# LayerNorm's reciprocal deviation on GpSimd, and more of the normalising on ScalarE

## The chip, the cores and the metric

The kernel runs on one core of one Trainium2 chip. The metric is the device time of one launch in microseconds, the median of several runs; the profile is of one further execution, and its span is a little shorter than the time. A core has five engines with instruction queues of their own: TensorE (PE: matmuls and weight loads), VectorE (DVE), ScalarE (ACT), GpSimd (POOL) and SyncE (SP, which here only issues DMAs). They meet through semaphores.

## The reference

The input x has 2048 tokens of 576 values. A LayerNorm (epsilon 1e-5) feeds a linear attention block with 32 heads of 18 channels; a gated feed-forward block of width 4608 works on the same normalised tokens, as the last lines say:

```
x = A_x
xn = _layernorm(x, axis=-1)
return x + _A_ref(xn, A_wqkv, A_wo) + _B_ref(xn, B_w_gate, B_w_up, B_w_down)
```

Attention computes q, k, v from xn, phi(t) = where(t > 0, t + 1, exp(t)) + 1e-6 for q and k, a 18x18 sum of phi(k) times v per head, the sum z of phi(k), and the quotient of the two products with phi(q), times wo. The change concerns only how (x - mean) / sqrt(var + eps) is made.

## The kernel before

The tokens lie as 16 tiles of 128. The work has three stages. The first, up to about 58 us of the profile, takes each tile through the LayerNorm, transposes it, multiplies it with the key and query weights, forms phi and adds the tile to a product G of xn and phi(k). A short second stage, up to 66.7 us, finishes the sums and the masked attention matrices. The third, to the end, is the feed-forward block with the attention output folded into its last product; it takes up the rest of the span and isn't touched.

The path of tile n in the first stage, by the names in the code:

- stats and aggr (L211, L214, VectorE): two halves of mean and variance, then joined into mv.
- rstd (`ln_rstd`, L216 to L219, ScalarE): 1/sqrt(var + eps) as exp(-0.5 ln(var + eps)), two activations on one value per partition.
- norm: on VectorE (`ln_norm`, L231) as (x - mean) * rstd; or on ScalarE (`ln_norm_act`, L226) as x * rstd + nbias, for which GpSimd first makes nbias = -mean * rstd (`ln_bias`, L221). Odd tiles from 3 on take ScalarE, the others VectorE.
- the transpose: tiles 0 and 1 go over PE (`transposes`, L244) in two parts, blocks 0 to 2 and blocks 3 and 4 of the 128 columns, each part with its own norm and its own copy back (`tp_copy`, L249, line L251). The later tiles take a DMA transpose issued by SP (`dma_transposes`, L253).
- mm, exp, phi (L262, L269, L274): per tile two halves of the key product and two of the query product, each five matmuls of 288 columns, an exponential on ScalarE and a combination on VectorE. A tile's product reuses the bank of the tile before, so it waits for that phi.
- z (`z_add`, GpSimd, L197) sums phi(k), and G (L293, PE) accumulates.

The order of the instructions on each engine is not written out by hand. Each of these is a step with an engine, a planned duration, a rank, and the steps that it follows; `in_order` (L482) plays the steps through with the planned durations and, among what could begin within 0.05 us, picks the lowest rank on that engine. So a planned duration or another engine moves instructions of other tiles as well. On the chip the queues then run strictly in that order, with the real durations.

Ahead of the steps, the loads are issued: tile 0 and 1 of x, the key weights (`load_w(1)`), two more tiles, the query weights (`load_w(0)`), four more tiles. PE runs 38 small products on an identity (`spin`) while it waits. GpSimd fills constants: padding of xn, ones in the bias rows, and the masks of the second stage (`bmask` L179 to L187, a part of `g_sb` L189, `ones` L192).

Of the kernel before, what the change touches and what calls it, by code (L numbers as in the profile page):

```python
# [8 lines left out]
ACT = mybir.ActivationFunctionType  # L9
ALU = mybir.AluOpType  # L10
BF16 = mybir.dt.bfloat16
F32 = mybir.dt.float32
# [3 lines left out]
P = 128  # L16
HP = 64
S = 2048
D = 576
H = 32  # L20
DH = 18
F = 4608
NS = S // P
# [5 lines left out]
KT = 5  # L29
# [4 lines left out]
EPS_LN = 1e-5  # L34
# [23 lines left out]
def kernel(  # L58
# [11 lines left out]
    nc = tc.nc  # L70
# [8 lines left out]
    const = ctx.enter_context(tc.tile_pool(name="const", bufs=1))  # L79
# [10 lines left out]
    x_sb = persist.tile([P, NS, D], BF16, name="x_sb")  # L90
# [28 lines left out]

    ident = const.tile([P, P], BF16, name="ident")  # L120
    make_identity(nc, ident[:])
    eps_ln = const.tile([P, 1], F32, name="eps_ln")
    nc.vector.memset(eps_ln[:], EPS_LN)
    eps_att = const.tile([P, 1], F32, name="eps_att")
    nc.vector.memset(eps_att[:], EPS_ATT)
    neg1 = const.tile([P, 1], F32, name="neg1")
    nc.vector.memset(neg1[:], -1.0)

    def spin(count):

        for _ in range(count):
            nc.tensor.matmul(ps_all[:, 7, 0:P], lhsT=ident[:], rhs=ident[:], start=True, stop=True)
# [19 lines left out]
    def load_gu(i, part):  # L152
# [17 lines left out]
    xn = apool.tile([P, NS, XW], BF16, name="xn")  # L170
# [4 lines left out]
    nc.gpsimd.memset(pk[:, :, D + 1:D + 2], 1.0)  # L175

    bmask = const.tile([P, CR], F32, name="bmask")
    bm3 = bmask[:].rearrange("p (h e) -> p h e", e=DH)
    nc.gpsimd.memset(bmask[:], 1.0)  # L179
    nc.gpsimd.affine_select(  # L180
        out=bm3, in_=bm3, compare_op=ALU.is_ge, fill=0.0,
        base=0, pattern=[[-DH, 7], [0, DH]], channel_multiplier=1,
    )
    nc.gpsimd.affine_select(
        out=bm3, in_=bm3, compare_op=ALU.is_ge, fill=0.0,
        base=DH - 1, pattern=[[DH, 7], [0, DH]], channel_multiplier=-1,
    )  # L187
    g_sb = apool.tile([P, KT, D], BF16, name="g_sb")
    nc.gpsimd.memset(g_sb[:, 4, :], 0.0)  # L189

    ones = const.tile([P, P], BF16, name="ones")
    nc.gpsimd.memset(ones[:], 1.0)  # L192
    z_sum = apool.tile([P, D], F32, name="z_sum")
    z_bf = apool.tile([P, D], BF16, name="z_bf")

# [6 lines left out]
    mv = persist.tile([P, NS, nc.vector.BN_AGGR_DIM], F32, name="mv")  # L202
    rstd = persist.tile([P, NS], F32, name="rstd")
    nbias = persist.tile([P, NS], F32, name="nbias")
# [3 lines left out]
    def ln_half(n, h):  # L208
        if h == 0:
            ln_raw[n] = asmall.tile([P, 2, nc.vector.BN_STATS_DIM], F32, name="stats")  # L210
        nc.vector.bn_stats(out=ln_raw[n][:, h, :], in_=x_sb[:, n, h * HALF:(h + 1) * HALF])  # L211

    def ln_aggr(n):
        nc.vector.bn_aggr(out=mv[:, n, :], in_=ln_raw[n][:])  # L214

    def ln_rstd(n):  # L216
        r = rstd[:, n:n + 1]
        nc.scalar.activation(out=r, in_=mv[:, n, 1:2], func=ACT.Ln, bias=eps_ln[:], scale=1.0)
        nc.scalar.activation(out=r, in_=r, func=ACT.Exp, scale=-0.5)  # L219

    def ln_bias(n):  # L221
        nc.gpsimd.tensor_scalar(
            out=nbias[:, n:n + 1], in0=mv[:, n, 0:1], scalar1=rstd[:, n:n + 1], scalar2=-1.0, op0=ALU.mult, op1=ALU.mult,
        )

    def ln_norm_act(n):  # L226
        nc.scalar.activation(
            out=xn[:, n, 0:D], in_=x_sb[:, n, :], func=ACT.Identity, bias=nbias[:, n:n + 1], scale=rstd[:, n:n + 1],
        )

    def ln_norm(n, c0=0, c1=D):  # L231
        nc.vector.tensor_scalar(
            out=xn[:, n, c0:c1], in0=x_sb[:, n, c0:c1], scalar1=mv[:, n, 0:1], scalar2=rstd[:, n:n + 1],
            op0=ALU.subtract, op1=ALU.mult,
        )
# [8 lines left out]
    def transposes(n, k0=0, k1=KT, b=None):  # L244
        b = TP_BANK[n] if b is None else b
        for kt in range(k0, k1):
            nc.tensor.transpose(tp_bank(b)[:, kt, :], xn[:, n, kt * P:(kt + 1) * P], ident[:])

    def tp_copy(n, k0=0, k1=KT, b=None, copy=acopy):  # L249
        b = TP_BANK[n] if b is None else b  # L250
        copy(out=xnT[:, k0:k1, n * P:(n + 1) * P], in_=tp_bank(b)[:, k0:k1, :])  # L251

    def dma_transposes(n):  # L253
        nc.sync.dma_start_transpose(xnT[:, :, n * P:(n + 1) * P], xn[:, n, 0:640])
# [4 lines left out]
    def kq_mm(n, which, hf):  # L259
        c = which * D + hf * HALF  # L260
        for kt in range(KT):
            nc.tensor.matmul(  # L262
                ps_all[:, KQ_BANK[which] + hf, :HALF], lhsT=xnT[:, kt, n * P:(n + 1) * P],
                rhs=wqkv_sb[:, kt, c:c + HALF], start=(kt == 0), stop=(kt == KT - 1),
            )

    def kq_exp(n, which, hf):
        e = e_tiles[n, which, hf] = awork.tile([P, HALF], F32, name="phi_e", tag="phi_e", bufs=8)
        nc.scalar.activation(  # L269
            out=e[:], in_=ps_all[:, KQ_BANK[which] + hf, :HALF], func=ACT.Exp, bias=neg1[:], scale=1.0,  # L270
        )
# [159 lines left out]
    def step(name, *args, **kw):  # L431
        steps[name] = _Step(*args, **kw)

    X_AT = [3.65, 4.20, 6.40, 6.40] + [9.50] * 4
    W_AT = {1: 5.50, 0: 7.60}

# [2 lines left out]
    for n in range(NS):  # L439
        lead = {0: -9.0, 1: 0.5, 2: -0.5, 3: -0.5}.get(n, 0.0)  # L440
        after_x = [("x", n // 2 * 2)] if n >= 8 else []
        x_at = X_AT[n] if n < 8 else 0.0
        for h in range(2):
            step(("stats", n, h), "DVE", 0.41, n - 2.2 + lead, after_x, lambda n=n, h=h: ln_half(n, h), ready=x_at)
        step(("aggr", n), "DVE", 0.21, n - 2.1 + lead, [("stats", n, 0), ("stats", n, 1)], lambda n=n: ln_aggr(n))
        step(("rstd", n), "ACT", 0.49, n - 2.1 + lead, [("aggr", n)], lambda n=n: ln_rstd(n))
        if n < TD:
            for i, (k0, k1, eng) in enumerate([(0, 3, "ACT"), (3, KT, "ACT" if n else "DVE")]):
                b = TP_BANK[n] - i
                step(("norm", n, i), "DVE", 0.25, n - 2.1 + lead, [("rstd", n)],  # L450
                     lambda n=n, k0=k0, k1=k1: ln_norm(n, k0 * P, min(k1 * P, D)))
                step(("tp", n, i), "PE", 0.20, n - 1.5 + lead, [("norm", n, i)],
                     lambda n=n, k0=k0, k1=k1, b=b: transposes(n, k0, k1, b))
                step(("xnT", n, i), eng, 0.30 if i else 0.48, n - 0.88 + lead, [("tp", n, i)],
                     lambda n=n, k0=k0, k1=k1, b=b, eng=eng: tp_copy(n, k0, k1, b, acopy if eng == "ACT" else vcopy))
            ready = [("xnT", n, 0), ("xnT", n, 1)]
        else:
            if n % 2:
                step(("bias", n), "POOL", 0.15, n - 2.1, [("rstd", n)], lambda n=n: ln_bias(n))
                step(("norm", n), "ACT", 0.65, n - 2.1, [("bias", n)], lambda n=n: ln_norm_act(n))  # L460
            else:
                step(("norm", n), "DVE", 0.43, n - 2.1, [("rstd", n)], lambda n=n: ln_norm(n))
            step(("xnT", n), "SP", 2.10, n - 1.9, [("norm", n)], lambda n=n: dma_transposes(n), tail=1.7)
            ready = [("xnT", n)]
        for which, rank in ((1, n), (0, n + 0.6)):
            for h in range(2):
                r = rank + h / 100
                free = [("phi", n - 1, which, h)] if n else []
                step(("mm", n, which, h), "PE", 0.615, r, ready + free, lambda n=n, w=which, h=h: kq_mm(n, w, h),
                     ready=W_AT[which], tail=0.15)  # L470
                step(("exp", n, which, h), "ACT", 0.49, r + 0.10, [("mm", n, which, h)],
                     lambda n=n, w=which, h=h: kq_exp(n, w, h))
                step(("phi", n, which, h), "DVE", 0.44, r + 0.15, [("exp", n, which, h)],
                     lambda n=n, w=which, h=h: kq_phi(n, w, h))
        if n > 0:
            idle = [("norm", n + 4) if n % 2 == 0 else ("bias", n + 4)] if n + 4 < NS else []
            step(("z", n), "POOL", 1.40, n + 2.0, [("phi", m, 1, h) for m in (0, n) for h in range(2)] + idle,
                 lambda n=n: z_add(n))
        step(("G", n), "PE", 0.75, n + 1.15, [("phi", n, 1, 0), ("phi", n, 1, 1)], lambda n=n: g_accumulate(n, G_A))
    step(("spin",), "PE", 0.11, -1.0, [("tp", 0, 1)], lambda: spin(2))  # L480

    def in_order(steps):  # L482

# [262 lines left out]
```

## Time and profile before

The time is 512.57 us, the median of 3 runs (512.55 to 512.6); the profile's span is 510.9 us.

| engine | busy us | share of the span | instructions |
|---|---|---|---|
| PE matmul | 505.0 | 99% | 4487 |
| PE weight load | 305.4 | 60% | 4487 |
| VectorE | 211.2 | 41% | 447 |
| ScalarE | 136.8 | 27% | 267 |
| GpSimd | 24.7 | 5% | 38 |

The operations that the change touches, in the first stage:

| line, engine | operation | count | mean ns |
|---|---|---|---|
| L218 ACT | Ln, 128x1 | 16 | 288 |
| L219 ACT | Exp, 128x1 | 16 | 203 |
| L222 POOL | nbias, 128x1 | 7 | 265 |
| L227 ACT | norm, 128x576 | 7 | 862 |
| L232 DVE | norm, 128x576 | 7 | 439 |
| L232 DVE | norm, 128x384 and 128x192 | 2 and 2 | 352 and 323 |
| L197 POOL | z sum, 128x576 | 13 | 1244 |

A matmul's reported length includes its way through the pipeline, so consecutive ones overlap; its cost to the next is the distance of their starts. The chain of work that ended last is followed back from the last instruction: at each step to what released it. What is busy beside that chain costs nothing. In a timeline line the first number is the start in us, the second the time that the group spans, and the bracket says how long the engine was idle before it and what ended that.

### The profile page before, as it was taken

The page shows a single profiled execution, that of the slowest core. Times are in us where ns is not written, and L with a number is a line of the kernel's source. Part 1 is how long each engine was busy: PE and PEld are TensorE (multiplying, and loading weights), DVE is VectorE, ACT ScalarE, POOL GpSimd, SP SyncE. Part 2 cuts the span into 40 slices and gives each one's busy share as a digit, 9 for nine tenths or more (in the row PEclk, how much of TensorE's full clock was granted, in tenths as well). Part 3 has the DMA queues.
Part 4 walks back from the last instruction along what each step waited for, and adds up shares of the span by engine and source line. Part 5 has one row for each costly group of instructions (what it writes and reads, how often), then busy time and mean ns, then how long its engine had stood idle before and what let it go on. Part 6 is the DMA issues. An engine that isn't in the chain of part 4 may idle for free.

```text
span 510.9 us, 10642 instructions
## 1 busy us (share of the span) xinstructions
PE 505.0 (99%) x4487; PEld 305.4 (60%) x4487; DVE 211.2 (41%) x447; ACT 136.8 (27%) x267; POOL 24.7 (5%) x38
## 2 busy tenths in 40 slices
PE   7999999999999999999999999999999999999997
PEld 6888854444587744444677644444777444445775
DVE  7887455555400045565200255555100356543100
ACT  5887533332310022332100023323000232232000
POOL 3344200000000000000000000000000000000000
PEclk9999999999999999999999999999999999999999
DMA  6643939999500067665300266567100565540000
GB/s 210 144 66 56 256 94 262 279 272 289 136 12 13 1 175 168 158 167 161 87 12 13 69 172 170 156 172 157 32 12 1 148 166 156 164 129 14 13 12 24
DMA packets 119002, 61.26 MB, mean 120 GB/s; under 512 B 25570, under 2 KB 118122, under 8 KB 118954
## 3 DMA queue, kind: packets, MB, share of 16 engines
q1 hardware_dynamic: 118810, 60.43, 45.3%
q8 instruction: 35, 0.57, 0.5%
q10 hardware_dynamic: 144, 0.15, 0.1%
q14 instruction: 13, 0.11, 0.1%
HBM read 52.86 MB, written 2.36 MB: 108 GB/s over the span
## 4 chain that ended last, share of the span: by engine, by line
PE 98%; DMA 1%; SPq 0%; DVE 0%; issue 0%
PE ps_all L324 55%; PE ps_all L668 28%; PE ps_all L262 7%; PE ps_all L293 3%; PE ps_all L673 3%; DMA wqkv_sb<-in_A_wqkv_dram 1%; PE ps_all L656 0%; PE ps_all L300 0%; PE ps_all L373 0%; PE ps_all L619 0%; SPq L93 0%; SPq L108 0%; DVE res L682 0%; SPq L107 0%; PE ps_all L361 0%
## 5 line engine op out<-in xcount | busy, mean ns | idle before, releaser
L324 PE MATMUL ps_all<-xnT,wg 64*128 64x512 bf16 x1152 | 271.9, 376 | 0.0
L324 PE MATMUL ps_all<-xnT,wu 64*128 64x512 bf16 x1152 | 271.5, 376 | 0.0
L608 ACT ACTIVATE gl<-ps_all 128x512 f32<-128x512 f32 x144 | 86.0, 597 | 311.1 <-PE ps_all L324 311.1
L609 DVE TENSOR_TENSOR hT<-ps_all,gl 128x512 bf16<-128x512 f32 x144 | 99.6, 691 | 131.2 <-ACT gl L608 130.7
L324 PEld LDWEIGHTS <-wu 64*128 64x128 bf16 x1152 | 108.3, 94 | 68.3
L324 PEld LDWEIGHTS <-wg 64*128 64x128 bf16 x1152 | 108.3, 94 | 67.7
L668 PE MATMUL ps_all<-wd_sb,hT 128*128 128x288 bf16 x1152 | 147.1, 286 | 0.0
L668 PEld LDWEIGHTS <-hT 128*128 128x128 bf16 x1152 | 112.3, 98 | 29.3 <-issue 1.2
L682 DVE TENSOR_TENSOR res<-ps_all,x_sb 128x288 bf16<-128x288 f32 x32 | 13.8, 455 | 146.4 <-PE ps_all L673 88.2
L324 PE MATMUL ps_all<-xnT,wr 64*128 64x512 bf16 x288 | 54.6, 376 | 0.0
L262 PE MATMUL ps_all<-wqkv_sb,xnT 128*128 128x288 bf16 x320 | 42.1, 286 | 0.5 <-ACT xnT L251 0.3
L262 PEld LDWEIGHTS <-xnT 128*128 128x128 bf16 x320 | 30.5, 98 | 7.9 <-ACT xnT L251 0.4
L269 ACT ACTIVATE phi_e<-ps_all,neg 128x288 f32<-128x288 f32 x64 | 30.9, 495 | 9.1 <-PE ps_all L262 6.3
L324 PEld LDWEIGHTS <-wr 64*128 64x128 bf16 x288 | 14.0, 94 | 16.8 <-issue 0.2
L673 PE MATMUL ps_all<-m_sb,pqT 128*128 128x288 bf16 x128 | 20.9, 286 | 0.0
L293 PE MATMUL ps_all<-hT,xn 128*128 128x288 bf16 (+4 forms) x144 | 18.8, 274 | 0.0
L274 DVE SCALAR_TENSOR_TENSOR pq<-phi_e,ps_all 128x288 bf16<-128x288 f32 x32 | 14.2, 449 | 7.7 <-ACT phi_e L269 7.4
L197 POOL TENSOR_TENSOR z_sum<-z_sum,hT 128x576 f32<-128x576 f32 x13 | 16.2, 1244 | 4.7 <-DVE hT L274 4.4
L293 PEld LDWEIGHTS <-xn 128*128 128x128 bf16 x144 | 14.0, 98 | 3.6 <-issue 0.2
L274 DVE SCALAR_TENSOR_TENSOR hT<-phi_e,ps_all 128x288 bf16<-128x288 f32 x32 | 14.1, 453 | 2.4 <-ACT phi_e L269 2.3
L673 PEld LDWEIGHTS <-pqT 128*128 128x128 bf16 x128 | 12.5, 98 | 3.2
L211 DVE BATCH_NORM_STATS2 stats<-x_sb 128x6 f32<-128x288 bf16 x32 | 13.6, 440 | 1.8 <-DMA x_sb<-in_A_x_dram 1.8
(62 smaller groups left out, 123.3 us busy)
## 6 DMA issues: line engine op xcount, KB each, us to landing
wg<-in_B_w_gate_dram SPq DMA_DIRECT2D x72, 256.0 KB, 2.9
wu<-in_B_w_up_dram SPq DMA_DIRECT2D x72, 256.0 KB, 3.5
wd_sb<-in_B_w_down_dram SPq DMA_DIRECT2D x12, 432.0 KB, 4.7
wr<-in_B_w_gate_dram SPq DMA_DIRECT2D x72, 32.0 KB, 2.8
wr<-in_B_w_up_dram SPq DMA_DIRECT2D x72, 32.0 KB, 3.0
out_dram<-res SPq DMA_DIRECT2D x15, 144.0 KB, 1.8
wqkv_sb<-in_A_wqkv_dram SPq DMA_DIRECT2D x3, 576.0 KB, 4.6
x_sb<-in_A_x_dram SPq DMA_DIRECT2D x5, 288.0 KB, 3.2
```

The lines of the kernel that those rows point to most:

```text
L197: nc.gpsimd.tensor_tensor(out=z_bf[:] if n == NS - 1 else z_sum[:], in0=pk[:, 0, 1:D + 1] if n == 1 else z_sum[:], in1=pk[:, n, 1:D + 1], ...
L211: nc.vector.bn_stats(out=ln_raw[n][:, h, :], in_=x_sb[:, n, h * HALF:(h + 1) * HALF])
L262: nc.tensor.matmul(ps_all[:, KQ_BANK[which] + hf, :HALF], lhsT=xnT[:, kt, n * P:(n + 1) * P], rhs=wqkv_sb[:, kt, c:c + HALF], start=(kt == ...
L269: nc.scalar.activation(out=e[:], in_=ps_all[:, KQ_BANK[which] + hf, :HALF], func=ACT.Exp, bias=neg1[:], scale=1.0,)
L274: nc.vector.scalar_tensor_tensor(out=(pq, pk)[which][:, n, which + hf * HALF:which + (hf + 1) * HALF], in0=e_tiles[n, which, hf][:], scala ...
L293: nc.tensor.matmul(ps_all[:, b, col:col + w], lhsT=xn[:, n, kt * P:(kt + 1) * P], rhs=pk[:, n, 1 + d0:1 + d0 + w], start=(n == 0 and col = ...
L324: return nc.tensor.matmul(self.outs[i], lhsT=self.lhs(i, rows, kt), rhs=self.rhs(i, rows, kt), start=start, stop=stop, skip_group_check=True,)
L608: nc.scalar.activation(out=gl[:], in_=ps_all[:, b[0], :], func=ACT.Gelu_apprx_tanh)
L609: nc.vector.tensor_tensor(out=hT[:, GUB * k + i, :], in0=ps_all[:, b[1], :], in1=gl[:], op=ALU.mult)
L668: nc.tensor.matmul(self.acc(hf), lhsT=hT[:, f, j * P:(j + 1) * P], rhs=wd_sb[:, f, HALVES[hf]], start=(f == 0 and not paired), stop=False, ...
L673: nc.tensor.matmul(self.acc(hf), lhsT=pqT[:, c, self.ts], rhs=m_sb[:, c, HALVES[hf]], start=False, stop=(paired and c == 3), skip_group_ch ...
L682: nc.vector.tensor_tensor(out=self.res[:, hs], in0=self.acc(hf), in1=x_sb[:, self.n, hs], op=ALU.add)
```

## The change

The reciprocal deviation is made by GpSimd: an addition of epsilon, and a power with the exponent -0.5 held in a column `mhalf`. ScalarE no longer has Ln and Exp to do. Which engine normalises a tile is now written out in `NORM` (D for VectorE, A for ScalarE): tile 1 goes to ScalarE in its two parts, and of the later tiles 3, 5, 6, 7, 9, 10, 12, 13 and 15. The masks and constants of the second stage become steps for GpSimd that follow the third tile's rstd. The planner gets new durations for these steps. The aim is to take small dependent work off ScalarE and VectorE, and to let the first tiles reach PE sooner.

In the order of the built program, PE has all five transposes of tile 1 ahead of the first query matmuls of tile 0; before, three stood ahead of them and two between their halves.

```diff
--- before.py
+++ after.py
@@ -119,10 +119,10 @@
 
     ident = const.tile([P, P], BF16, name="ident")
     make_identity(nc, ident[:])
-    eps_ln = const.tile([P, 1], F32, name="eps_ln")
-    nc.vector.memset(eps_ln[:], EPS_LN)
     eps_att = const.tile([P, 1], F32, name="eps_att")
     nc.vector.memset(eps_att[:], EPS_ATT)
+    mhalf = const.tile([P, 1], F32, name="mhalf")
+    nc.vector.memset(mhalf[:], -0.5)
     neg1 = const.tile([P, 1], F32, name="neg1")
     nc.vector.memset(neg1[:], -1.0)
 
@@ -175,21 +175,25 @@
     nc.gpsimd.memset(pk[:, :, D + 1:D + 2], 1.0)
 
     bmask = const.tile([P, CR], F32, name="bmask")
-    bm3 = bmask[:].rearrange("p (h e) -> p h e", e=DH)
-    nc.gpsimd.memset(bmask[:], 1.0)
-    nc.gpsimd.affine_select(
-        out=bm3, in_=bm3, compare_op=ALU.is_ge, fill=0.0,
-        base=0, pattern=[[-DH, 7], [0, DH]], channel_multiplier=1,
-    )
-    nc.gpsimd.affine_select(
-        out=bm3, in_=bm3, compare_op=ALU.is_ge, fill=0.0,
-        base=DH - 1, pattern=[[DH, 7], [0, DH]], channel_multiplier=-1,
-    )
     g_sb = apool.tile([P, KT, D], BF16, name="g_sb")
-    nc.gpsimd.memset(g_sb[:, 4, :], 0.0)
-
     ones = const.tile([P, P], BF16, name="ones")
-    nc.gpsimd.memset(ones[:], 1.0)
+
+    def make_bmask():
+        bm3 = bmask[:].rearrange("p (h e) -> p h e", e=DH)
+        nc.gpsimd.memset(bmask[:], 1.0)
+        nc.gpsimd.affine_select(
+            out=bm3, in_=bm3, compare_op=ALU.is_ge, fill=0.0,
+            base=0, pattern=[[-DH, 7], [0, DH]], channel_multiplier=1,
+        )
+        nc.gpsimd.affine_select(
+            out=bm3, in_=bm3, compare_op=ALU.is_ge, fill=0.0,
+            base=DH - 1, pattern=[[DH, 7], [0, DH]], channel_multiplier=-1,
+        )
+
+    def clear_g():
+        nc.gpsimd.memset(g_sb[:, 4, :], 0.0)
+        nc.gpsimd.memset(ones[:], 1.0)
+
     z_sum = apool.tile([P, D], F32, name="z_sum")
     z_bf = apool.tile([P, D], BF16, name="z_bf")
 
@@ -215,17 +219,17 @@
 
     def ln_rstd(n):
         r = rstd[:, n:n + 1]
-        nc.scalar.activation(out=r, in_=mv[:, n, 1:2], func=ACT.Ln, bias=eps_ln[:], scale=1.0)
-        nc.scalar.activation(out=r, in_=r, func=ACT.Exp, scale=-0.5)
+        nc.gpsimd.tensor_scalar_add(out=r, in0=mv[:, n, 1:2], scalar1=EPS_LN)
+        nc.gpsimd.tensor_tensor(out=r, in0=r, in1=mhalf[:], op=ALU.pow)
 
     def ln_bias(n):
         nc.gpsimd.tensor_scalar(
             out=nbias[:, n:n + 1], in0=mv[:, n, 0:1], scalar1=rstd[:, n:n + 1], scalar2=-1.0, op0=ALU.mult, op1=ALU.mult,
         )
 
-    def ln_norm_act(n):
+    def ln_norm_act(n, c0=0, c1=D):
         nc.scalar.activation(
-            out=xn[:, n, 0:D], in_=x_sb[:, n, :], func=ACT.Identity, bias=nbias[:, n:n + 1], scale=rstd[:, n:n + 1],
+            out=xn[:, n, c0:c1], in_=x_sb[:, n, c0:c1], func=ACT.Identity, bias=nbias[:, n:n + 1], scale=rstd[:, n:n + 1],
         )
 
     def ln_norm(n, c0=0, c1=D):
@@ -431,6 +435,9 @@
     def step(name, *args, **kw):
         steps[name] = _Step(*args, **kw)
 
+    NORM = "DADADAAADAADAADA"
+    COPY = ("DVE", "ACT")
+    POW = 0.55
     X_AT = [3.65, 4.20, 6.40, 6.40] + [9.50] * 4
     W_AT = {1: 5.50, 0: 7.60}
 
@@ -443,19 +450,25 @@
         for h in range(2):
             step(("stats", n, h), "DVE", 0.41, n - 2.2 + lead, after_x, lambda n=n, h=h: ln_half(n, h), ready=x_at)
         step(("aggr", n), "DVE", 0.21, n - 2.1 + lead, [("stats", n, 0), ("stats", n, 1)], lambda n=n: ln_aggr(n))
-        step(("rstd", n), "ACT", 0.49, n - 2.1 + lead, [("aggr", n)], lambda n=n: ln_rstd(n))
+        step(("rstd", n), "POOL", POW, n - 2.1 + lead, [("aggr", n)], lambda n=n: ln_rstd(n))
         if n < TD:
-            for i, (k0, k1, eng) in enumerate([(0, 3, "ACT"), (3, KT, "ACT" if n else "DVE")]):
+            for i, (k0, k1, eng) in enumerate([(0, 3, "ACT"), (3, KT, COPY[n])]):
                 b = TP_BANK[n] - i
-                step(("norm", n, i), "DVE", 0.25, n - 2.1 + lead, [("rstd", n)],
-                     lambda n=n, k0=k0, k1=k1: ln_norm(n, k0 * P, min(k1 * P, D)))
+                if NORM[n] == "A":
+                    if not i:
+                        step(("bias", n), "POOL", 0.15, n - 2.1 + lead, [("rstd", n)], lambda n=n: ln_bias(n))
+                    step(("norm", n, i), "ACT", (0.49, 0.36)[i], n - 2.1 + lead, [("bias", n)],
+                         lambda n=n, k0=k0, k1=k1: ln_norm_act(n, k0 * P, min(k1 * P, D)))
+                else:
+                    step(("norm", n, i), "DVE", (0.27, 0.20)[i], n - 2.1 + lead, [("rstd", n)],
+                         lambda n=n, k0=k0, k1=k1: ln_norm(n, k0 * P, min(k1 * P, D)))
                 step(("tp", n, i), "PE", 0.20, n - 1.5 + lead, [("norm", n, i)],
                      lambda n=n, k0=k0, k1=k1, b=b: transposes(n, k0, k1, b))
                 step(("xnT", n, i), eng, 0.30 if i else 0.48, n - 0.88 + lead, [("tp", n, i)],
                      lambda n=n, k0=k0, k1=k1, b=b, eng=eng: tp_copy(n, k0, k1, b, acopy if eng == "ACT" else vcopy))
             ready = [("xnT", n, 0), ("xnT", n, 1)]
         else:
-            if n % 2:
+            if NORM[n] == "A":
                 step(("bias", n), "POOL", 0.15, n - 2.1, [("rstd", n)], lambda n=n: ln_bias(n))
                 step(("norm", n), "ACT", 0.65, n - 2.1, [("bias", n)], lambda n=n: ln_norm_act(n))
             else:
@@ -473,11 +486,14 @@
                 step(("phi", n, which, h), "DVE", 0.44, r + 0.15, [("exp", n, which, h)],
                      lambda n=n, w=which, h=h: kq_phi(n, w, h))
         if n > 0:
-            idle = [("norm", n + 4) if n % 2 == 0 else ("bias", n + 4)] if n + 4 < NS else []
+            idle = [("norm" if NORM[n + 4] == "D" else "bias", n + 4)] if n + 4 < NS else []
             step(("z", n), "POOL", 1.40, n + 2.0, [("phi", m, 1, h) for m in (0, n) for h in range(2)] + idle,
                  lambda n=n: z_add(n))
         step(("G", n), "PE", 0.75, n + 1.15, [("phi", n, 1, 0), ("phi", n, 1, 1)], lambda n=n: g_accumulate(n, G_A))
     step(("spin",), "PE", 0.11, -1.0, [("tp", 0, 1)], lambda: spin(2))
+
+    step(("bmask",), "POOL", 0.95, 0.2, [("rstd", 2)], make_bmask)
+    step(("g",), "POOL", 0.75, 0.3, [("rstd", 2)], clear_g)
 
     def in_order(steps):
```

## The prediction

> **What bounds the kernel now.** I read the page's busy shares first, then the chain that ended last, then the stages by window, then the timeline of the first ten microseconds. TensorE (PE) is busy 99% of the span, and the chain that ended last is 98% PE, so anything on another engine counts only where it makes PE wait. The windows say where that is. Columns: the stretch in us, its length, then PE, weight loads, VectorE, ScalarE and GpSimd busy time with counts, clock, DMA share, GB/s.
>
> ```profile
> 5.10:6.74 1.64, 0.64 (x7) 0.40 (x8) 1.38 (x7) 0.76 (x4) 0.36 (x2) 1.00 1.05 372
> 6.74:8.55 1.81, 1.57 (x14) 1.14 (x15) 1.74 (x7) 1.29 (x6) 0.00 (x0) 1.00 1.09 367
> 9.43:20.00 10.57, 10.57 (x91) 8.55 (x90) 9.55 (x27) 9.28 (x25) 2.70 (x4) 1.00 0.48 106
> 20.00:30.00 10.00, 10.00 (x87) 8.12 (x85) 9.15 (x28) 8.01 (x21) 3.78 (x6) 1.00 0.64 125
> 40.00:50.00 10.00, 10.00 (x86) 8.10 (x85) 7.01 (x19) 8.29 (x20) 5.34 (x6) 1.00 0.31 51
> ```
>
> From 9.43 to the feed-forward part PE has no idle time at all, although VectorE and ScalarE are busy 70 to 95% there. Time can be won or lost ahead of 9.43, or by a new gap later. The chain in order of time (start, length, what) shows what releases PE:
>
> ```profile
> 2.95 5.56 DMA wqkv_sb<-in_A_wqkv_dram
> 8.50 0.04 issue
> 8.55 0.77 PE ps_all L262 x5
> 9.32 0.11 PE ps_all L247 x2
> 9.43 1.84 PE ps_all L262 x15
> ```
>
> The query weights land at 8.50; five query matmuls of tile 0 start at 8.55; then two transposes of tile 1 (0.11 us) stand in the chain; then all is matmul. Behind 8.55 PE's work is fixed, so the end is 8.55 plus that work. The timeline shows tile 0 and 1 on their way there:
>
> ```profile
> 4.58 0.21 DVE L214 BATCH_NORM_AGGREGATE mv<-stats 128x2 f32<-128x12 f32 x1
> 4.83 0.30 ACT L218 ACTIVATE rstd<-mv,eps_ln 128x1 f32<-128x1 f32 x1 [2.31 <-DVE mv L214]
> 5.16 0.20 ACT L219 ACTIVATE rstd<-rstd 128x1 f32<-128x1 f32 x1
> 5.39 0.62 DVE L232 TENSOR_SCALAR xn<-x_sb,mv,rstd 128x384 bf16<-128x384 bf16 x2
> 5.93 0.20 DVE L214 BATCH_NORM_AGGREGATE mv<-stats 128x2 f32<-128x12 f32 x1
> 6.74 1.40 PE L262 MATMUL ps_all<-wqkv_sb,xnT 128*128 128x288 bf16 x10 [0.28 <-ACT xnT L251]
> 7.57 0.56 DVE L232 TENSOR_SCALAR xn<-x_sb,mv,rstd 128x384 bf16<-128x384 bf16 x2
> 7.98 0.33 PE L247 MATMUL ps_all<-ident,xn 128*128 128x128 bf16 x3
> ```
>
> Tile 1 was aggregated at 6.13, but its norm started only at 7.57, behind tile 2's statistics on VectorE. Hence only three of its five transposes fit before 8.55.
>
> **What the Trainium skill says.** (1) "ScalarE: Activation LUTs", section "What ACT_TABLE_LOAD costs": an ACTIVATE with a pointer bias takes about 280 ns + 0.833 ns per element, another pointer operand adds 93, neighbours overlap by 93. For the norm with two pointers and 576 columns that is 853 ns; the trace has 862, so it agrees. (2) "GPSIMD Engine Reference", section 3.1: a two-input operation costs about 2.6 cycles per element, at 1.2 GHz. The z sum over 576 columns would be 1.25 us by that; the trace has 1.244. It states no price for a power. (3) "Perfetto Trace Analysis", section "GPSIMD Engine Instruction": reported GpSimd spans are unreliable, start-to-start is better. Here the bias reads 0.265 us, yet the z sum behind it starts 0.22 after it. (4) "SBUF — State Buffer", section "Who interferes with whom": a VectorE tensor_scalar in a 2-port mode and a GpSimd operation exclude each other. The trace fits: the norm of 128x576 takes mostly 0.43 us, and 0.57 beside a z sum.
>
> **The change, part by part.**
>
> *Removed:* 16 pairs Ln+Exp on ScalarE, start to end 0.53 us each (4.83 to 5.36), 8.5 us of ScalarE. Behind 9.43 this is worth nothing: PE has no gap there. *Moved:* norms of tiles 6, 10 and 12 from VectorE (0.43) to ScalarE (0.86, 0.77 start to start), also behind 9.43 and hidden by PE; ScalarE nets about -6 us. *The masks* (1.7 us on GpSimd, 3.75 to 5.46) go behind the third rstd. They are read only at the mask product and the z product, about 66 us; hidden by 50 us of PE work. They cost the fourth tile's rstd a wait, treated below.
>
> *rstd on GpSimd.* Two instructions with a semaphore wait between them. The trace has no power. Lower bound: two of the cheapest 128x1 operations (memset, 0.10) with the 0.07 hand-off seen in the bmask chain: 0.27. Nearest row: the bias, 0.265, for each: 0.265+0.065+0.265 = 0.60. Upper bound: the page's two-input price says nothing of a function evaluated in software; for a power of about 1 us I take 1.4. I call the pair r and take 0.60, since one column leaves little but the fixed cost.
>
> *Tile 0's chain:* aggregate ends 4.79, GpSimd starts 4.83 and ends 4.83+r; before it was 5.36. So tile 0 shifts by d = r-0.53, 0.07 with my value. Its key matmuls start at 6.74+d and finish ten issues of 0.123 us at 7.97+d.
>
> *Tile 1's chain* (now on ScalarE): aggregate 6.13+d; rstd ends 6.17+d+r; bias with its hand-offs 0.065+0.265, ScalarE starts 0.04 later, at 6.54+d+r. What is queued behind these norms on ScalarE: two exps of tile 0, then the copies of tile 1's transposes. Norm halves by the page's formula (an estimate): 384 columns 0.69, next start 0.60 later, 192 columns 0.53, so the end is 1.13 later: 7.67+d+r. PE sees it 0.07 later and issues the last two transposes in 0.11. All five transposes now stand ahead of the first query matmul, so that matmul starts at the later of 8.55 (the weights, whose load isn't changed) and 7.85+d+r = 7.32+2r. With r = 0.60 this is 8.52, just inside. The two transposes then lie in the wait for the weights, and 0.11 us leaves the chain. Up to r = 0.615 the gain is the full 0.11; each 0.1 more costs 0.2; it breaks even at 0.67.
>
> *Behind that:* tile 1's copies end near 9.9 and its key matmuls need them from 9.78 (first three blocks, ready near 9.5) and 10.15: no stall. Tile 2: norm on VectorE at about 8.5, ends 8.92, DMA transpose issued 9.0, landing 2.6 us later at 11.6; PE needs it at 11.75 (11.86 less 0.11). That is tight, as before (9.06+2.6 = 11.66 against 11.86). Tile 3: rstd waits for the masks until about 10.2; norm 11.2 to 12.07, landing 14.7, needed 14.95; before it landed near 14.94 against 15.06. Tile 5's norm moves from 17.79 to about 17.1. GpSimd per tile: 0.60 + about 0.33 + 1.24 = 2.2 us of the 3.2 us that PE spends on a tile, so it holds.
>
> *Sum:* -0.11 us; 512.57 - 0.11 = 512.46, called 512.5.
>
> **The rivals.**
> - *The power costs more* (r from 0.67 to 1.18): the loss is 2r-1.34, from 0 to 1.0 us; at r = 0.9 it is 512.57+0.46 = 513.0. For it: a function of two operands in software. Against it: one element per partition, the rest of such rows is 0.1 to 0.27 us.
> - *The power is slow* (r over 1.18), and slower than before by over 0.2%: at r = 1.4 the loss is 1.46, 514.0; with r near 2 GpSimd reaches the 3.2 us per tile and becomes the bound. For it: no row and no page prices the operation. Against: it needs a power above 0.85 us, three times the bias.
> - *A late tile:* tile 2 or 3 misses its slack of 0.15 to 0.25 and PE stalls once, 0.1 to 0.4 us; 512.7. For it: the thin slack, and masks beside VectorE's norm. Against: ScalarE and VectorE both have less to do.
> - *A real gain* over 0.2% (1.03 us) would need the query weights earlier; their issue at 2.95 and the DMA share near 1.0 ahead of 8.55 aren't touched. About 511.5.
>
> **How the numbers follow.** My case 55%, costlier power 25%, slow power 12%, late tile 6%, real gain 2%. The time is that of my case, 512.5. Low end 512.3: the full gain, with the 0.05 us between runs and a little between chips; high end 513.4: r up to 1.1, which holds most of the second case and the fourth. Over 0.2% faster 2%; slower 13% (slow power and the edge of the second case); within it 85%.
>
> **What would show it.** In the chain of the changed kernel: the query weights' DMA still the piece before the first query matmul at 8.55, no transposes behind it. In GpSimd's timeline: start of the add to the end of the power 0.60. In ScalarE's: two norm pieces of tile 1 near 7.2 to 8.35. PE idle from there to 67 us: none. If the piece before the query matmuls is a transpose waiting for ScalarE's norm, the power was dearer; if a gap stands near 11.8 or 15, a tile came late; if GpSimd is busy all through, it became the bound.

## The result and the profile after

The changed kernel takes 514.88 us (median of 4 runs, 514.36 to 515.72) against 512.56 on the same chip: 2.3 us more, ratio 1.0048 with a 95% interval of 1.003 to 1.0065. The forecast was 512.5 with a range of 512.3 to 513.4, so the result lies outside. Its four runs stand on two levels, 514.36 and 514.38, 515.38 and 515.72, where the kernel before had all four within 0.25. The profiled run is one of the upper level.

TensorE now has idle time ahead of the feed-forward part. The page's head, and the share of each engine in the chain that ended last (98% PE before):

```profile
span 513.7 us, 10671 instructions
PE 507.6 (99%) x4487; PEld 306.8 (60%) x4487; DVE 211.3 (41%) x443; ACT 133.2 (26%) x239; POOL 38.3 (7%) x73
PE 93%; DVE 3%; POOL 1%; issue 1%; DMA 1%; ACT 1%; ACTq 0%
```

The first feed-forward matmul starts at 69.35, before at 66.61. These 2.74 us are nearly the whole 2.8 by which the span grew (510.9 to 513.7). A ruler between the two ends is the start of each tile's G matmuls (a G block), whose distance was 3.20 us before, up to the fifteenth. Some of these lines, before and after; those between are left out:

```profile
11.11 0.91 PE L293 MATMUL ps_all<-hT,xn 128*128 128x288 bf16 x7
27.11 0.92 PE L293 MATMUL ps_all<-hT,xn 128*128 128x288 bf16 x7
39.92 0.92 PE L293 MATMUL ps_all<-hT,xn 128*128 128x288 bf16 x7
```

```profile
12.61 0.91 PE L297 MATMUL ps_all<-hT,xn 128*128 128x288 bf16 x7
28.62 0.92 PE L297 MATMUL ps_all<-hT,xn 128*128 128x288 bf16 x7
32.15 0.92 PE L297 MATMUL ps_all<-hT,xn 128*128 128x288 bf16 x7
35.35 0.92 PE L297 MATMUL ps_all<-hT,xn 128*128 128x288 bf16 x7
38.95 0.91 PE L297 MATMUL ps_all<-hT,xn 128*128 128x288 bf16 x7
42.66 0.92 PE L297 MATMUL ps_all<-hT,xn 128*128 128x288 bf16 x7
```

In the changed kernel the first starts at 12.61 instead of 11.11 (**1.50 lost in the front**), and three distances, 28.62 to 32.15, 35.35 to 38.95 and 38.95 to 42.66, are longer by 0.33, 0.40 and 0.51 (**1.24 lost later**).

The front, by the chain in order of time (start, length, what):

```profile
5.05 0.24 POOL rstd L222
5.29 0.07 issue
5.36 0.58 POOL rstd L223
5.94 0.03 issue
5.97 0.39 DVE xn L236
6.36 0.05 issue
6.40 0.52 PE ps_all L251 x3
6.94 0.49 ACT xnT L255
7.43 0.05 issue
7.48 2.57 PE ps_all L266 x10
10.04 0.28 PE ps_all L251 x5
10.32 2.45 PE ps_all L266 x20
```

The DMA of the query weights is no longer the piece ahead of the query matmuls. The chain now comes from tile 0's statistics through both GpSimd instructions. From the add's start at 5.05 to the power's end at 5.94 are **0.89 us, not 0.60**; the power alone is 0.57. And the ten key matmuls of tile 0 take 2.57 us where the same ten took 1.40 before. The timeline of the changed kernel shows two paces of one row:

```profile
1.41 4.23 PE L132 MATMUL ps_all<-ident 128*128 128x128 bf16 x38 [1.41 <-POOL ident masks.py:199]
6.40 0.71 PE L251 MATMUL ps_all<-ident,xn 128*128 128x128 bf16 x5 [0.76 <-DVE xn L236]
7.48 2.57 PE L266 MATMUL ps_all<-wqkv_sb,xnT 128*128 128x288 bf16 x10
10.16 2.12 PE L266 MATMUL ps_all<-wqkv_sb,xnT 128*128 128x288 bf16 x16
```

At 7.48 one key matmul comes every 0.24 us, at 10.16 one every 0.12. Nothing waits in between: the array runs at half pace until about 10. The granted clock that the page prints is full all through.

The later loss, by the waits of ScalarE from 12 to 50 us (in total, times, longest). The kernel before had none for nbias:

```profile
ACT xn L231 <- POOL nbias L226: 5.2, 8, 1.2
ACT phi_e L273 <- PE ps_all L266: 2.5, 4, 1.2
```

One stall followed back, by the timeline of all engines:

```profile
28.16 0.21 DVE L218 BATCH_NORM_AGGREGATE mv<-stats 128x2 f32<-128x12 f32 x1
28.46 0.22 POOL L222 TENSOR_SCALAR rstd<-mv 128x1 f32<-128x1 f32 x1 [1.23 <-DVE mv L218]
28.77 0.57 POOL L223 TENSOR_TENSOR rstd<-rstd,mhalf 128x1 f32<-128x1 f32 x1
29.44 0.27 POOL L226 TENSOR_SCALAR nbias<-mv,rstd 128x1 f32<-128x1 f32 x1
29.74 0.87 ACT L231 ACTIVATE xn<-x_sb,nbias,rstd 128x576 bf16<-128x576 bf16 x1 [1.03 <-POOL nbias L226]
30.51 1.26 ACT L273 ACTIVATE phi_e<-ps_all,neg 128x288 f32<-128x288 f32 x3
31.03 0.46 DVE L278 SCALAR_TENSOR_TENSOR hT<-phi_e,ps_all 128x288 bf16<-128x288 f32 x1 [0.64 <-ACT phi_e L273]
31.54 0.77 PE L266 MATMUL ps_all<-wqkv_sb,xnT 128*128 128x288 bf16 x5 [0.17 <-DVE hT L278]
```

ScalarE's norm stands in its queue, 1.03 us idle, for a bias that GpSimd could not make sooner: from the aggregate's end at 28.37 to the bias's end at 29.71 are 1.34 us, where the order was written for 0.55 + 0.15 = 0.70. Behind the norm stand exponentials that don't depend on it. They come late, VectorE's phi products with them, then PE. GpSimd is idle 1.23 us ahead of this, so it isn't overloaded; each tile's chain through it is too long for the order. The aggregate at 28.16 is late itself, and GpSimd's z sums have a part in that: the tile before was aggregated at 24.54, but its add stood behind a z sum until 25.18, and its norm on VectorE, at 26.33, took 1.06 us beside the next z sum, ahead of the statistics that the aggregate needs.

So the theory had three parts: (a) the length of the power in front; (b) a low TensorE clock in some of the runs, because PE is idle too long between the spin and tile 0's transposes; (c) an order planned for a shorter power. The experiments take them one at a time. Times are medians with the range of the runs, ratios are to the kernel before (512.6 to 512.7) on the same chip.

### The profile page after: what moved, and what is told of

Same layout as the page of the kernel before. It is cut to its first block, busy times and chain, and to the rows that moved or that the text cites. A ratio compares the mean times of both kernels' runs of the same rounds, so it can differ in the third digit from the quotient of the medians.

```text
span 513.7 us, 10671 instructions
## 1 busy us (share of the span) xinstructions
PE 507.6 (99%) x4487; PEld 306.8 (60%) x4487; DVE 211.3 (41%) x443; ACT 133.2 (26%) x239; POOL 38.3 (7%) x73
## 4 chain that ended last, share of the span: by engine, by line
PE 93%; DVE 3%; POOL 1%; issue 1%; DMA 1%; ACT 1%; ACTq 0%
PE ps_all L328 54%; PE ps_all L684 28%; PE ps_all L266 4%; PE ps_all L689 3%; PE ps_all L297 2%; DVE pq L278 1%; DVE stats L215 1%; DVE hT L278 1%; DMA x_sb<-in_A_x_dram 1%; DVE xn L236 1%; ACT phi_e L273 0%; POOL z_sum L201 0%; PE ps_all L672 0%; POOL rstd L223 0%; PE ps_all L304 0%
## 5 line engine op out<-in xcount | busy, mean ns | idle before, releaser
L266 PE MATMUL ps_all<-wqkv_sb,xnT 128*128 128x288 bf16 x320 | 43.7, 291 | 0.7 <-DVE pq L278 0.2
```

The source lines that it names most:

```text
L266: nc.tensor.matmul(ps_all[:, KQ_BANK[which] + hf, :HALF], lhsT=xnT[:, kt, n * P:(n + 1) * P], rhs=wqkv_sb[:, kt, c:c + HALF], start=(kt == ...
```

## The experiments

**1. Ln and Exp back on ScalarE for all tiles but tile 2.** The new norms and the masks' place stay.

```diff
...
+        if n != 2:
+            nc.scalar.activation(out=r, in_=mv[:, n, 1:2], func=ACT.Ln, bias=eps_ln[:], scale=1.0)
+            nc.scalar.activation(out=r, in_=r, func=ACT.Exp, scale=-0.5)
+            return
...
+        eng_r, took_r = ("ACT", 0.49) if n != 2 else ("POOL", POW)
...
```

> The changed kernel with Ln and Exp on ScalarE again for all tiles but tile 2; the split of the norms and the place of the masks stay changed. Theory (the loss comes from the power on GpSimd, in three parts: its latency in front of tile 0 and 1, about 0.45 us; a cold TensorE clock in some runs, about 1.1 us; stalls around tiles 8 to 11, about 1.2 us): all three go, 512.4 to 512.7. Rival (the split of the norms and the new order cost the time): stays at 514.3 or more.

Measured 513.55 (512.89 to 514.57, 20 runs), ratio 1.0016 [1.0009, 1.0023]. Both expectations missed: the power makes most of the loss, not all. The later loss is gone (from the second G block at 14.99 to the fifteenth at 56.61 are 41.62 us, as before), so the split of norms and the masks cost nothing there. In front 0.69 us stay. Tile 1 is now on ScalarE, and there its Ln waits behind the copy of tile 0's transposes, then comes the bias on GpSimd, then the norm: the first query matmul starts at 8.83 instead of 8.55. The other 0.4 us are lost between there and the second G block; what PE waits for there isn't shown. The profiled run, 513.36, has the fast key matmuls; what holds the ten runs above 513.6 isn't shown either.

**2 and 3. One half of that each**: Ln and Exp for tiles 0 and 1 only (`if n < 2`), or for tiles 2 and later only (`if n >= 2`).

> Ln and Exp on ScalarE for tiles 0 and 1 alone, the power for the others. Theory: the front part and the cold clock go, the stalls at tiles 8 to 11 stay: 513.6 to 513.9, TensorE gaps of together 1.2 us between 28 and 44 us. Rival (all of the loss is the latency of the power ahead of the first query matmul): 512.5.

Measured 514.29 (514.03 to 514.64, 8 runs), ratio 1.0031 [1.002, 1.0041]: 0.4 above the expectation. In front 0.48 us are lost (G of tile 1 at 14.78), later 0.88, not the whole 1.2; ScalarE waits for nbias 4.6 us in 5 waits. Power on the later tiles alone brings the later stalls.

> The power for tiles 0 and 1 alone, Ln and Exp on ScalarE for the others. Theory: the front part stays, the later stalls go: 513.0 where the TensorE clock is up, 514.1 where it is cold. Rival (all of the loss is the latency in front): as the changed kernel, 514.4 to 515.7.

Measured 514.45 (514.3 to 515.06, 6 runs), ratio 1.0035 [1.0023, 1.0046]. The later loss is gone as said (16.05 to 57.67 is 41.62), but the front loses 1.75, more than was expected: the first query matmul is at 9.29, then PE waits 0.33 for the copies of tile 1's transposes, and at 14.81 it waits 0.43, where tile 2's DMA transpose has landed 4.7 us after its issue (the median of the fourteen is 2.6). Why that one is late stays open. The trace places the losses here; the total falls in the rival's range and alone would mislead.

**4. A longer spin in the changed kernel**, to close the idle time ahead of tile 0's transposes.

```diff
-NWARM = 38
+NWARM = 50
```

> The changed kernel with 50 small products in front in place of 38. Theory (the idle gap of TensorE ahead of tile 0's transposes, now later by 0.6 us, lets the clock stay low in some runs): the key matmuls of tile 0 are 0.12 us apart in every run and the runs agree, 514.3 to 514.5. Rival (two levels of time have another cause): runs still spread from 514.4 to 515.7.

Measured 515.04 (514.96 to 515.11, 4 runs), ratio 1.0042 [1.0026, 1.0059].

```profile
1.41 4.88 PE L132 MATMUL ps_all<-ident 128*128 128x128 bf16 x50 [1.41 <-POOL ident masks.py:199]
7.22 1.40 PE L266 MATMUL ps_all<-wqkv_sb,xnT 128*128 128x288 bf16 x10 [0.28 <-ACT xnT L255]
14.25 1.40 PE L266 MATMUL ps_all<-wqkv_sb,xnT 128*128 128x288 bf16 x10 [0.35 <-DMA xnT<-xn]
```

Ten key matmuls take 1.40 again, and the runs agree within 0.15. Yet the time is 0.5 above the expectation: PE waits at 14.25 for tile 2's DMA transpose, which again lands 4.6 us after its issue. So the clock's part was open until experiments 11 and 12. The spin itself tells more: its products come every 0.107 us up to 5.44 and every 0.055 from 5.52 on (in experiment 11, too), that is from the 40th product. A spin of 38 that is slow to its last product, as in the changed kernel, ends just ahead of this point.

**5. The z sums of tiles 2 to 14 left out.**

```diff
-        if n > 0:
+        if n in (1, NS - 1):
```

> The changed kernel with the z sums of tiles 2 to 14 left out (so z is only tile 0, 1 and 15; this is part of the computation). In the changed kernel TensorE loses 1.24 us between its 6th and 10th G block (28.62 to 42.66 us against 27.11 to 39.92 before). Theory (VectorE's norms of tiles 8 and 11, 1.06 and 1.55 us in place of 0.43, are held back by GpSimd's z sum at the shared port, and late biases hold up ScalarE): without z the norms take 0.43 us, the G blocks keep 3.20 us distance, and the time is about 1.2 us under the changed kernel. Rival (the power alone delays the tiles there): gaps of 1 us or more remain.

Measured 513.34 (513.1 to 514.59, 12 runs), ratio 1.002 [1.0011, 1.0029]. All G distances are 3.20, and ScalarE waits for nbias 1.1 us instead of 5.2. So the later loss needs GpSimd's z sums (the planner writes its order without them, too). But they do two things: they stand in GpSimd's queue ahead of the next rstd, and they go with longer VectorE norms (0.42 here; 1.55 in the changed kernel at 34.43, beside a z sum of 1.29 at 34.52). Experiment 6 takes the second away, at the price of two more norms that wait for a bias.

**6. Two of VectorE's norms moved to ScalarE** (tiles 8 and 11).

```diff
-    NORM = "DADADAAADAADAADA"
+    NORM = "DADADAAAAAAAAADA"
```

> The changed kernel with tiles 8 and 11 normalised on ScalarE too, so that no VectorE norm meets a z sum there. Port theory: the loss between the 6th and 10th G block falls from 1.24 to under 0.4 us. Rival (ScalarE stands still for a late bias, with exponentials queued behind it): it stays at 1 us or grows, since two more norms wait for a bias.

Measured 515.38 (514.69 to 515.96, 4 runs), ratio 1.0052 [1.0035, 1.0069]. The later loss grew to about 1.4, and its first part (5th to 7th G block, 25.69 to 32.84) comes with no VectorE norm beside a z sum. So a loss there doesn't need the shared port; how much the port adds in the changed kernel this run can't tell, since it adds two waits for a bias. ScalarE's waits for the bias, in the same columns as above, grew:

```profile
ACT xn L231 <- POOL nbias L226: 6.7, 10, 2.2
```

**7. Nothing but the planner's number for the power**: the order that it writes changes, no instruction does.

```diff
-    POW = 0.55
+    POW = 0.95
```

> The changed kernel with 0.95 in place of 0.55 as the planned duration of the rstd pair, which took 0.89 us in the trace. Theory (the later stalls come from an order written for a shorter pair): most of the 1.24 us there goes, the front stays, 513.2 to 514.4. Rival (GpSimd's work and the port hold it up in any order): the loss there stays over 1 us.

Measured 513.13 (512.88 to 514.48, 12 runs; all but two within 512.88 to 513.17), ratio 1.0012 [1.0004, 1.0021]. **The later loss is gone**: from the third G block to the fifteenth every distance is 3.20 (the new order moves the second block forward; first to third are 6.40). The median lies a little below the expected range, because the new order shortens the front as well (experiment 11). Two windows of 20 to 60 us, first the changed kernel, then this one (length, then PE, weight loads, VectorE, ScalarE, GpSimd):

```profile
20.00:60.00 40.00, 39.47 (x329) 31.49 (x327) 30.63 (x79) 28.08 (x57) 25.74 (x41) 1.00 0.55 129
```

```profile
20.00:60.00 40.00, 40.00 (x340) 32.46 (x339) 30.60 (x80) 29.17 (x58) 25.68 (x39) 1.00 0.65 143
```

GpSimd is busy 25.7 us in both, VectorE 30.6 in both; PE has idle time in one of them alone. Load doesn't tell them apart, order does. ScalarE's timeline with the new order, at the place of the stall that was followed above:

```profile
29.53 0.85 ACT L231 ACTIVATE xn<-x_sb,nbias,rstd 128x576 bf16<-128x576 bf16 x1
30.50 1.73 ACT L273 ACTIVATE phi_e<-ps_all,neg 128x288 f32<-128x288 f32 x3
32.12 0.86 ACT L231 ACTIVATE xn<-x_sb,nbias,rstd 128x576 bf16<-128x576 bf16 x1
```

No wait stands before the norms: three exponentials go ahead of the next one, whose bias was ready at 31.16. From 12 to 50 us ScalarE waits for nbias 1.5 us instead of 5.2. A VectorE norm of 1.50 us beside a z sum is still in this trace, at 35.22, without a gap on PE.

**8. The norms' old split with the power** (`NORM = "DDDADADADADADADA"`, as the kernel before had it).

> The power on GpSimd and the later masks, with the split of the norms as before (tile 1 on VectorE, odd tiles from 3 on ScalarE). Theory: tile 0 shifts by 0.4 us as in the changed kernel, tile 1 gains the bias and ScalarE's slower norm back, so the front loss is 0.3 to 0.5 us; more VectorE norms meet z sums, so the later loss is 1 us or more; 513.8 to 514.6. Rival (the new split is what costs): 512.6 to 513.2.

Measured 514.02 (513.71 to 514.37, 7 runs), ratio 1.0027 [1.0016, 1.0038], in the expected range, but by luck: in the trace the front loses 0.58 (second G block at 14.88), more than the 0.3 to 0.5 expected, and the later part 0.46, less than half of the 1 us expected. GpSimd makes seven biases here instead of ten; whether that is why the later loss is smaller isn't shown.

**9. A multiplication in the power's place**, in the same order on every engine.

```diff
-    nc.vector.memset(mhalf[:], -0.5)
+    nc.vector.memset(mhalf[:], 20.0)
...
-        nc.gpsimd.tensor_tensor(out=r, in0=r, in1=mhalf[:], op=ALU.pow)
+        nc.gpsimd.tensor_tensor(out=r, in0=r, in1=mhalf[:], op=ALU.mult)
```

> The changed kernel with a multiplication in place of the power on GpSimd (the reciprocal deviation is left out, a scaled variance takes its place); the order of all instructions is the same. Theory (the mis-sized term is the power's 0.57 us; the order was written for a short pair): the pair takes 0.55 to 0.65 us, as the prediction took it, and with it both losses go, in front and between the 6th and 10th G block: 512.4 to 512.8. Rival (the place of the work and of the masks costs, whatever the power takes): 513.5 or more.

Measured 512.6 (512.39 to 514.43, 12 runs; eight of them up to 512.65), ratio 1.0003 [0.9994, 1.0012]. GpSimd's timeline:

```profile
5.08 0.22 POOL L222 TENSOR_SCALAR rstd<-mv 128x1 f32<-128x1 f32 x1 [1.20 <-DVE mv L218]
5.38 0.19 POOL L223 TENSOR_TENSOR rstd<-rstd,mhalf 128x1 f32<-128x1 f32 x1
```

and PE's:

```profile
6.96 1.40 PE L266 MATMUL ps_all<-wqkv_sb,xnT 128*128 128x288 bf16 x10 [0.28 <-ACT xnT L255]
8.19 0.61 PE L251 MATMUL ps_all<-ident,xn 128*128 128x128 bf16 x5
8.64 2.61 PE L266 MATMUL ps_all<-wqkv_sb,xnT 128*128 128x288 bf16 x20
```

This is the prediction's own case: a pair of 0.49 us, all five transposes ahead of the query matmuls, no gap up to the feed-forward part (66.60), no difference to the kernel before. With this order, 0.38 us of one instruction make all the rest.

**10. Ln and Exp for tiles 0 and 1, power for the others, planned at 0.95.**

> Ln and Exp for tiles 0 and 1, the power for tiles 2 to 15 with 0.95 as its planned duration. Theory (in front the power costs its latency, later only the order written for a shorter pair): the kernel before within 0.3 us, 512.4 to 512.9, with G blocks 3.20 us apart. Rival (the power costs time later in any order): 513.4 or more.

Measured 512.84 (512.63 to 513.22, 12 runs), ratio 1.0002 [0.9993, 1.0011]: no difference that the runs resolve; the trace has 0.25 in front (second G block at 14.55) and 3.20 between all blocks. A power on fourteen tiles is free once the order knows its length.

**11. The plan at 0.95 and 50 small products in the spin.**

> The changed kernel with 0.95 as planned duration and 50 small products. The runs of that plan with 38 products stood at 513.1 and at 514.2 to 514.6, and the profiled one at the upper level had key matmuls of tile 0 at 0.24 us. Theory (the upper level is the low TensorE clock, which outlasts the idle gap ahead of tile 0's transposes): all runs at 513.1 to 513.3. Rival (the levels have another cause): both levels again.

Measured 513.11 (513.0 to 513.59, 12 runs), ratio 1.0008 [0.9999, 1.0016]. One level; the highest run is 0.9 below the highest with 38 products (514.48). What is left is the power's length in front, and less of it than in the first order: the third G block starts at 17.98, in experiment 5 at 18.21, before at 17.51. (The main levels of experiments 5 and 7, 513.2 and 513.1, differ in the same way.) With the longer plan VectorE aggregates tile 1 at 5.61, while it would wait for tile 0's power, and not at 6.46 behind tile 0's norms (experiment 5); and PE has half of tile 0's key matmuls, then tile 1's transposes:

```profile
7.25 0.79 PE L266 MATMUL ps_all<-wqkv_sb,xnT 128*128 128x288 bf16 x5 [0.28 <-ACT xnT L255]
7.96 0.72 PE L251 MATMUL ps_all<-ident,xn 128*128 128x128 bf16 x5
```

**12. The kernel before with a shorter spin** (`NWARM` 38 to 30): a shorter warm-up, and with it more idle time ahead of its own tile 0.

> The kernel before with 30 small products in place of 38, so that TensorE is idle for some 0.6 us longer ahead of tile 0's transposes, with nothing else changed. Theory of the low clock: the key matmuls of tile 0 are 0.24 us apart in some or all runs, the first query matmul then comes up to 0.7 us late, 512.6 to 513.4. Rival (a gap of this length doesn't matter): 512.5 in all runs.

Measured 513.43 (512.28 to 514.25, 20 runs: ten from 512.28 to 513.09, ten from 513.76 to 514.25), ratio 1.0013 [1.0005, 1.002]. The profiled run took 514.23:

```profile
1.43 3.38 PE L132 MATMUL ps_all<-ident 128*128 128x128 bf16 x30 [1.43 <-POOL ident masks.py:199]
5.78 0.71 PE L247 MATMUL ps_all<-ident,xn 128*128 128x128 bf16 x5 [0.97 <-DVE xn L232]
6.85 2.58 PE L262 MATMUL ps_all<-wqkv_sb,xnT 128*128 128x288 bf16 x10
9.55 1.30 PE L262 MATMUL ps_all<-wqkv_sb,xnT 128*128 128x288 bf16 x5
```

The slow pace comes without any power: the key matmuls at 0.24 us, and here five query matmuls, too (1.30; 0.77 before), so more than the 513.4 that was allowed. Whether the shorter spin or the longer gap does it, this run doesn't separate; between the kernel before and the changed one the spin has the same 38 products, and the gap grew.

No version beats the kernel before; 9, which doesn't compute the deviation, and 10 equal it within the intervals.

## Why the prediction was wrong

**Right.** Where the bound lies (the way to 8.55, no gap behind it); that the five transposes move ahead of the query matmuls; that the masks and the moved norms are hidden; ScalarE's two halves, 1.13 estimated and 1.14 measured; and the sum 7.32+2r for the first query matmul: with r = 0.88 to 0.89 it gives 9.08 to 9.10, measured 9.31 in experiment 4 and 9.36 in 5, at the full clock. The 0.2 between is mostly the hand-offs (0.08 where 0.04 was put) and tile 0's statistics, which started at 3.62 to 4.03 from profile to profile (3.73 in the kernel before, 3.81 in experiment 4, 3.86 in 5). Before, the weights' landing at 8.50 hid that scatter.

**Wrong, the step that failed: "I call the pair r and take 0.60".** The nearest row was the bias, 0.265 for each of the two instructions. The add fits (0.22), the power takes 0.57, so r is 0.88. The bounds 0.27 and 1.4 held it; the choice between them rested on the row of another operation, and 0.60 is also a value at which the case still gains. In front the power costs 0.65 to 0.70 in this order: at the full clock the first G block starts at 11.76 (experiment 4) and 11.81 (5), against 11.11. The rival of a costlier power had put 2r-1.34 = 0.42 for it: its mechanism is the one that the front shows, its total of 513.0 at r = 0.9 is short of the result, because it had neither of the next two. Experiment 9 shows that with r = 0.49 the time is the forecast's within the noise; of the gain of 0.11 its trace has 0.02 (first G block at 11.09 against 11.11).

**Wrong, and in no case of the prediction: "GpSimd per tile: 2.2 us of the 3.2 us, so it holds".** The real load, 0.88 + 0.36 + 1.24 = 2.5 us, still fits; the conclusion doesn't follow. What counts here is when a result comes, and what stands in a queue behind those who wait for it. The prediction had named the exponentials queued on ScalarE for tile 1, and not looked for them at the later tiles. Lost: 1.24 us, all of it given back by one number in the plan (experiment 7). Three things have to meet for this loss, and taking any one away ends it: the power's length (9), the z sums (5) and the order written for a shorter pair (7).

**Wrong by omission: the clock.** "Ten issues of 0.123 us" was taken over to a kernel in which the spin and the transposes stand differently. The key matmuls took 0.24 apiece in all four profiled runs of an upper level (the changed kernel, experiments 6, 7 and 12), and 0.12 in the other ten profiles. Ten of them lose 10 times 0.117, 1.2 us, but not all of it reaches the end: at the full clock PE waits some 0.3 us for tile 1 behind them (experiment 5: the tenth comes near 8.4, the transposes at 8.80). The Trainium skill, "TensorE: Matmul & The Clock Gate", section "Part 1: The HAM clock gate", says that the array starts at half rate, is released after some 3.4 us of sustained work as seen by a free-running window, and that the moment varies from run to run. The traces agree in the two paces and in the scatter: the spin's products sped up at 4.27 (before), at 4.38 (experiment 5) or only near 5.5 (4 and 11), which is 2.8 to 4.1 us after its start, on both sides of the page's 3.4. They show that the gap alone doesn't decide it. Where the spin's 38 products sped up before their end (3.62 to 3.80 us in all), the key matmuls ran at full rate even after a gap of 1.26 (experiment 5; 0.78 in the kernel before). Where they were slow to the last (4.23 in all, one every 0.107), a gap of 0.40 or 0.47 to the transposes did no harm (experiments 9 and 8), and one of 0.67 to 0.76 left the key matmuls slow (experiments 6 and 7, the changed kernel). With 50 products no run among 16 stood on a second level, with 30 half of 20 did; these counts go by the times, one run of each kernel was profiled. After a slow spin the kernel before would, by estimate, have a gap of some 0.17 left (transposes at 5.83, a slow spin's end at 1.43+4.23 = 5.66); the dearer pair stretches it to 0.76. That the window's phase picks the runs is the page's reading; no run here shows the window itself.

The profiled run of the upper level adds up: 0.7 for the power, 0.8 for the slow pace (first G block at 12.61 against 11.81 in experiment 5) and 1.24 later are 2.74, measured 515.38, that is 2.8 above; the lower level 0.7 + 1.24 = 1.9, measured 1.8. How long the slow pace lasts isn't the same in each run: in experiment 6 the first G block is at 12.89, with the same front. So the other upper run, 515.72, can be a longer one; it has no profile.

**Open.** Why tile 2's transpose landed 4.2 to 4.7 us after its issue in experiments 1, 3, 4, 8 and 11 and 2.7 in the other nine profiles (PE waits where it lands only in 3 and 4); and what sets the moment at which the spin speeds up.

## What to carry to other kernels

An operation that no row and no page prices is a reason to forecast between its bounds and to widen the range, not to take the nearest row; here 0.3 us of it decided everything. A hand-written or planned order is part of the cost of an instruction: when one instruction in a chain across queues that run in order gets longer, look on each engine for what stands behind those who wait, and give the planner the measured length before judging the change. And a warm-up spin is fitted to the gap behind it; a shift of some 0.4 us in the first tile can leave the first matmuls at half pace, which the granted clock on the page doesn't show.

## What the runs showed of the hardware

- GpSimd on 128x1: power of two operands 0.57 us, multiplication 0.19, add of a constant 0.22; 0.08 to 0.10 between two of its own dependent instructions, 0.08 to 0.09 from VectorE's aggregate to its add.
- TensorE at the low pace: 0.24 us per 288-column matmul instead of 0.123, for 2.6 us (changed kernel) to 3.8 us (experiment 12) from the first key matmul on, after a spin of 3.4 to 4.2 us that was slow to its last product and a gap of 0.7 to 1.0 us, with a granted clock of 1.00 on the page. The same small product came every 0.107 us, and every 0.055 once the spin had sped up, 2.8 to 4.1 us after its start.
- A DMA transpose of one tile: median 2.6 to 3.0 us from issue to landing in every profile, but the slowest of the fourteen took 3.5 us (the kernel before) to 5.9 (experiment 1).
- VectorE's norm of 128x576 took 0.42 with no z sum beside it, and up to 1.55 us when it started within 0.1 us of a z sum of 1.29; the prediction's 0.57 beside a z sum was the mild case.
